# Attention through inducing points with a fused expert layer: a shared maximum per group, exp read from PSUM, a running maximum, and a list scheduler for the order of the work

## The chip, the core and the metric

The kernel runs on one core of a Trainium2 chip. Its engines are TensorE (PE, matrix products; the loads of its weights are listed as PEld), VectorE (DVE), ScalarE (ACT), GpSimd (POOL) and SyncE (SP, which issues DMAs). [...] The metric is the device time of one execution in microseconds (us); less is better.

## The reference

```python
B, N, C, m = 4, 11456, 128, 32        # x: (B, N, C), inducing: (m, C), float32
def mab(q, kv):
    s = q @ kv.T / sqrt(C)
    a = exp(s - s.max(-1)); a /= a.sum(-1) + 1e-9
    return a @ kv
h   = mab(inducing, x)                # first softmax: 32 queries over N tokens, per batch
y   = mab(x, h)                       # second softmax: each token over the 32 rows of h
e   = argmax(y @ w_gate)              # 8 experts, F = 1024 hidden units
out = softmax(y @ w_gate)[e] * (relu(y @ w1[e]) @ w2[e])     # per token
```

A token's `y` is a positive mixture of the 32 rows of `h`. Where every row agrees on the expert and on the sign of each hidden unit, relu(y @ w1[e]) @ w2[e] is linear in the mixture, and one 32x128 matrix per batch (`h4`) replaces the expert. The kernel tests this token by token (a sum of the second softmax's weights against a threshold `thr`) and counts the tokens that fail.

## The kernel before

The tokens of a batch lie in 4 quarters (q), each cut into 90 blocks of 32; 15 blocks of all four quarters make a group (a tile of 128 partitions x 480 columns), 6 groups a batch, 24 groups in all. Of each group the kernel loads `xt` (tokens along the columns, 0.98 MB, L180) and `xn` (tokens along the partitions, L186); for three groups of batch 0 it makes `xn` out of `xt` on TensorE (`turn_xn`). Both loads are issued by SP, the results (0.98 MB a group) by ACT (L496).

First softmax, per group: `attend1` multiplies `xt` with the inducing points into PSUM (L117, four column tiles), DVE transposes the scores in 32x32 blocks into SBUF (L217) and takes their maximum (L218). After all six groups `maxima` joins the maxima (two products) into one per inducing point. Then `attend2` subtracts it (L245, POOL; DVE for batch 0), takes exp (L249, ACT) and sums with 15 products (L258) into one bank `hp` over the whole batch. `induced` divides, finds the expert, and gathers its `w1` and `w2` by an indirect DMA of POOL (L310); `fused` makes `h4` (64 + 256 instructions of small products, L331, L353) and `thr`.

Second softmax, per group k: `scores` (L117); `less_max` (transpose L404, maximum of each token L406, subtraction on POOL L407); `exps` (L412); `logits` (transpose back L416, one product L418 with a matrix that gives the sum of the weights and the gate sums); `turn_logits` (L424). Per pair of groups, `gate1` to `gate3` alternate between POOL and DVE with one exp on ACT (L431 to L465) and give a factor per token. Then `weigh` multiplies (L470, POOL), `experts` transposes (L475) and multiplies with `h4` (L479, four row tiles into four banks `o`), and `evict` copies the four banks (L493, ACT) and stores.

The order is written by hand: `put(at, fn)` places each step at a tick; a group takes STEP = 6 ticks, `attend1` of batch b+2 and `attend2` of batch b+1 are laid between the groups of batch b, and `induced(0)` with its `fused` and the first `attend1` of batch 1 run before tick 0. At the end the failed tokens are counted (L600 to L613); a slow pass over them follows only if there are any.

Of the kernel before, what the change touches and what calls it, by code (L numbers as in the profile page):

```python
# [29 lines left out]
P = 128  # L31
# [4 lines left out]
GB = 15  # L36
# [17 lines left out]
def attn_moe_kernel(ctx, tc, xT, xn, indT, wg, w1, w2, consts, out):  # L54
# [20 lines left out]
    done_all = const.tile([P, B, NBLK], F32, name="done_all")  # L75
# [10 lines left out]
    def open_pools(st, rest):  # L86

        pl = Pools()

        def pool(name, bufs, **kw):  # L90
            return st.enter_context(tc.tile_pool(name=("r_" if rest else "m_") + name, bufs=bufs, **kw))

        pl.xt = pool("xt", 1 if rest else NXT)
        pl.e2 = pool("e2", 2 if rest else 4)
        pl.et = pool("et", 2)
        pl.small = pool("small", 2)
        pl.wraw = pool("wraw", 1)
        pl.fe = pool("fe", 2, space=PSUM)
        pl.mi = pool("mi", 1, space=PSUM)
        if rest:  # L100
            pl.z = pool("z", 2, space=PSUM)
            pl.o = pool("o", 2, space=PSUM)
            pl.ob = pool("ob", 2)
            pl.hid = pool("hid", 2)
        else:
            pl.hp = pool("hp", 1, space=PSUM)
            pl.o = pool("o", 4, space=PSUM)
            pl.lv = pool("lv", 2)
            pl.xn = pool("xn", 3)
            pl.s1 = pool("s1", 7)  # L110
        return pl


    def score_mm(pl, lhsT, xt_g):
        ps = pl.fe.tile([P, 512], F32, name="fe")
# [4 lines left out]
        return ps  # L120

    def softmax_exp(pl, hT, xt_g, side):

        ps = score_mm(pl, hT[:, 0:M], xt_g)
# [44 lines left out]
    pl = open_pools(main, False)  # L169

# [4 lines left out]
    for s in S:  # L175
        s.xt, s.xn, s.s1 = {}, {}, {}

    def load_xt(b, g):
        t = pl.xt.tile([P, GB, NQ, 32], F32, name="xt")
        nc.sync.dma_start(t, xT[b, g])  # L180
        S[b].xt[g] = t

    def load_xn(b, g, pool=pl.xn):

        t = pool.tile([P, GB, P + 1], F32, name="xn")
        nc.sync.dma_start(t, xn[b, :, g * GB : (g + 1) * GB, :])  # L186
        S[b].xn[g] = t

    def turn_xn(b, g, pool):

        s = S[b]
        t = pool.tile([P, GB, P + 1], F32, name="xn")
        nc.gpsimd.memset(t[:, :, P : P + 1], 1.0)
        s.xn[g] = t
        for k0 in range(0, GB, 4):
            n = min(4, GB - k0)
            ps = pl.o.tile([P, 512], F32, name="o")
            for k in range(n):
                nc.tensor.transpose(
                    ps[:, k * P : (k + 1) * P], s.xt[g][:, k0 + k].rearrange("p q t -> p (q t)"), ident  # L200
                )
            src = ps[:, : n * P].rearrange("p (k c) -> p k c", c=P)
            if k0 % 8 == 0 or b > 0:
                nc.scalar.copy(t[:, k0 : k0 + n, 0:P], src)
            else:
                nc.vector.tensor_copy(t[:, k0 : k0 + n, 0:P], src)
            yield

    def attend1(b, g):

        s = S[b]
        ps = score_mm(pl, it_sb, s.xt[g])
        yield
        if g == 0:
            s.mx1 = pl.small.tile([P, NG], F32, name="mx1")
        s.s1[g] = pl.s1.tile([P, GW], F32, name="s1")
        nc.vector.transpose(s.s1[g], ps[:, :GW])  # L217
        nc.vector.tensor_reduce(s.mx1[:, g : g + 1], ps[:, :GW], AX.X, ALU.max)  # L218

    def maxima(b):  # L220

        s = S[b]
        m1 = pl.small.tile([P, 1], F32, name="m1")
        nc.vector.tensor_reduce(m1, s.mx1, AX.X, ALU.max)
        mq = pl.small.tile([P, NQ], F32, name="mq")
        nc.vector.tensor_scalar_mul(mq, qmask, m1)
        ps = pl.mi.tile([P, 512], F32, name="mi")
        nc.tensor.matmul(ps[:, :NQ], lhsT=fold, rhs=mq, start=True, stop=True)
        yield
        mm = pl.small.tile([P, 1], F32, name="mm")  # L230
        nc.vector.tensor_reduce(mm, ps[:, :NQ], AX.X, ALU.max)
        dg = pl.small.tile([32, 32], F32, name="dg")
        nc.vector.tensor_scalar_mul(dg, ident[:32, :32], mm[:32])
        ps2 = pl.mi.tile([P, 512], F32, name="mi")
        nc.tensor.matmul(ps2[:, :32], lhsT=ones[:32, :], rhs=dg, start=True, stop=True)
        yield
        s.m1b = pl.small.tile([P, 32], F32, name="m1b")
        nc.vector.tensor_copy(s.m1b, ps2[:, :32])  # L238

    def attend2(b, g):  # L240

        s = S[b]
        e1 = blk(s.s1[g])
        side = nc.vector if b == 0 else nc.gpsimd
        side.tensor_tensor(  # L245
            out=e1, in0=e1, in1=s.m1b.unsqueeze(1).to_broadcast([P, GB, 32]), op=ALU.subtract
        )
        yield
        nc.scalar.activation(s.s1[g], s.s1[g], AF.Exp, scale=SCALE)  # L249
        if g == NG - 1:  # L250
            nc.gpsimd.memset(e1[64:128, GB - 1, :], 0.0)
        yield
        if g == 0:
            s.hp = pl.hp.tile([P, 512], F32, name="hp")
        for k in range(GB):
            n = g * GB + k
            j = n % 4
            nc.tensor.matmul(  # L258
                s.hp[32 * j : 32 * j + 32, : P + 1],
                lhsT=e1[:, k, :],  # L260
                rhs=s.xn[g][:, k, :],
                start=(n < 4),
                stop=(n >= NBLK - 4),
            )

    def induced(b):

        s = S[b]
        t = pl.small.tile([P, P + 1], F32, name="hsum")
        nc.scalar.copy(t, s.hp[:, : P + 1])  # L270
        ps = pl.mi.tile([P, 512], F32, name="mi")
        nc.tensor.matmul(ps[:, 0:1], lhsT=fold, rhs=t[:, P : P + 1], start=True, stop=True)
        yield
        rv = pl.small.tile([P, 1], F32, name="rv")
        nc.vector.tensor_scalar_add(rv, ps[:, 0:1], EPS)
        nc.vector.reciprocal(rv, rv)
        nc.vector.tensor_scalar_mul(t[:, :P], t[:, :P], rv)
        ps2 = pl.mi.tile([P, 512], F32, name="mi")
        nc.tensor.matmul(ps2[:, 0:P], lhsT=t[:, :P], rhs=fold, start=True, stop=True)
        yield  # L280
        nc.vector.tensor_copy(hT_all[:, b, :], ps2[:, 0:P])
        ps3 = pl.mi.tile([P, 512], F32, name="mi")
        nc.tensor.matmul(ps3[:, 0:E], lhsT=hT_all[:, b, :], rhs=wg_sb, start=True, stop=True)
        yield
        gs = pl.small.tile([P, E], F32, name="gs")
        nc.vector.tensor_copy(gs, ps3[:, 0:E])
        ps4 = pl.mi.tile([P, 512], F32, name="mi")
        nc.tensor.matmul(ps4[:, 0:E], lhsT=ones, rhs=gs, start=True, stop=True)
        yield

        cs = pl.small.tile([P, E], F32, name="cs")
        nc.vector.tensor_copy(cs, ps4[:, 0:E])
        cm = pl.small.tile([P, 1], F32, name="cm")
        nc.vector.tensor_reduce(cm, cs, AX.X, ALU.max)
        t2 = pl.small.tile([P, E], F32, name="t2")
        nc.vector.scalar_tensor_tensor(
            out=t2, in0=cs, scalar=cm, in1=val8, op0=ALU.is_ge, op1=ALU.mult
        )
        r1 = pl.small.tile([P, 1], F32, name="r1")
        nc.vector.tensor_reduce(r1, t2, AX.X, ALU.max)  # L300
        ix = pl.small.tile([P, 1], F32, name="ix")
        nc.vector.scalar_tensor_tensor(
            out=ix, in0=r1, scalar=-128.0, in1=pcol, op0=ALU.mult, op1=ALU.add
        )
        ii = pl.small.tile([P, 1], I32, name="ii")
        nc.vector.tensor_copy(ii, ix)
        s.w1r = pl.wraw.tile([P, F], F32, name="w1r")
        s.w2r = pl.wraw.tile([P, F], F32, name="w2r")
        for dst, src in ((s.w1r, w1), (s.w2r, w2)):
            nc.gpsimd.indirect_dma_start(  # L310
                out=dst, out_offset=None, in_=src, in_offset=bass.IndirectOffsetOnAxis(ap=ii[:, :1], axis=0)
            )

        oh = pl.small.tile([P, E], F32, name="oh")
        nc.vector.tensor_tensor(out=oh, in0=val8, in1=r1.to_broadcast([P, E]), op=ALU.is_equal)
# [78 lines left out]
    for k in range(0, B * NG, 2):  # L394
        K[k].pair = K[k + 1].pair = Pair()

# [404 lines left out]
```

## Time and profile before

| | before |
|---|---|
| three timed runs | 314.4 us median (312.33 to 315.57) |
| profiled execution | 311.58 us |
| its span, first to last instruction | 309.6 us |
[...]

The page names busy time of engines, which says nothing yet of who waits for whom; the timeline and the tables of waits do. A product of float32 appears as two instructions, so the four products of a group's scores are eight rows. Times in the timeline count from the span's start.

### The profile page before, as it was taken

How to read it: one execution, taken by the hardware profiler on the slowest of the kernel's cores; microseconds unless marked ns; L12 is line 12 of the kernel's file. 1: busy time of each engine (PE TensorE's matmuls, PEld its weight loads, DVE VectorE, ACT ScalarE, POOL GpSimd, SP SyncE). 2: the span in 40 equal slices, each digit the busy share in tenths (PEclk: the TensorE clock that was granted, in tenths of full speed). 3: DMA queues.
4: the chain of work that ended last, by engine and by line, in shares of the span. 5: the costliest groups of instructions: out<-in, count | busy, mean ns of one | idle time of the engine just before them, and what ended most of it. 6: DMA issues, size and time to landing. Idle time of an engine off the chain costs nothing. (4 is left out here: it accounts for less than half of the span.)

```text
span 309.6 us, 4648 instructions
## 1 busy us (share of the span) xinstructions
PE 231.7 (75%) x1771; PEld 106.8 (35%) x1772; DVE 153.3 (50%) x392; ACT 86.5 (28%) x172; POOL 117.5 (38%) x194
## 2 busy tenths in 40 slices
PE   2877725778397779769894899799876995994870
PEld 0536404145032145434421344255332541221330
DVE  0585250853656655633856427533544736545420
ACT  1314000023123041452251320362240601552451
POOL 0000020148513712962616403983535226717510
PEclk9995975899789568776999559756968576597555
DMA  7999994128929985757999531059163330345156
GB/s 288 423 420 421 415 416 196 43 89 300 423 67 377 381 326 211 239 197 309 385 371 385 169 163 60 0 188 386 68 255 125 135 131 2 127 176 207 48 227 244
DMA packets 11549, 72.72 MB, mean 235 GB/s; under 512 B 1536, under 2 KB 1664, under 8 KB 11520
## 3 DMA queue, kind: packets, MB, share of 16 engines
q1 hardware_dynamic: 6480, 44.40, 37.2%
q10 hardware_dynamic: 3888, 23.75, 18.7%
q0 software_dynamic: 1152, 4.19, 3.9%
q8 instruction: 16, 0.26, 0.4%
q14 instruction: 13, 0.11, 0.1%
HBM read 48.75 MB, written 23.59 MB: 234 GB/s over the span
## 5 line engine op out<-in xcount | busy, mean ns | idle before, releaser
L479 PE MATMUL o<-ec,h 32*128 32x480 f32 x192 | 63.6, 897 | 17.9 <-DVE ec L475 12.1
L493 ACT COPY ob<-o 128x480 f32<-128x480 f32 x96 | 48.1, 564 | 57.6 <-PE o L479 54.4
L407 POOL TENSOR_TENSOR e<-e,mx 128x480 f32<-128x480 f32 x24 | 23.8, 993 | 70.3 <-DVE mx L406 46.7
L117 PE MATMUL fe<-xt,it_sb 128*32 128x480 f32 x192 | 35.1, 713 | 8.4 <-DMA it_sb<-in_indT 5.8
L418 PE MATMUL mi<-et,gzb 128*128 128x480 f32 x48 | 32.3, 761 | 10.6 <-DVE et L416 5.8
L117 PE MATMUL fe<-xt,hT_all 128*32 128x480 f32 x192 | 38.8, 642 | 1.2 <-DVE mx L218 0.9
L479 PEld LDWEIGHTS o<-ec,h 32*128 32x128 f32 x192 | 22.9, 259 | 46.4 <-ACT ob L493 21.5
L258 PE MATMUL hp<-xn,s 128*32 128x129 f32 x720 | 32.9, 322 | 4.5 <-ACT s L249 2.5
L258 PEld LDWEIGHTS hp<-xn,s 128*32 128x32 f32 x720 | 26.5, 129 | 20.4 <-issue 10.4
L217 DVE STREAM_TRANSPOSE s<-fe 128x480 f32<-128x480 f32 x24 | 16.2, 675 | 28.6 <-PE fe L117 28.6
L416 DVE STREAM_TRANSPOSE et<-e 128x480 f32<-128x480 f32 x24 | 16.0, 669 | 20.3 <-ACT e L412 20.2
L475 DVE STREAM_TRANSPOSE ec<-e 128x480 f32<-128x480 f32 x24 | 16.1, 673 | 16.5 <-POOL e L470 16.5
L412 ACT ACTIVATE e<-e 128x480 f32<-128x480 f32 x24 | 14.6, 607 | 34.1 <-POOL e L407 34.1
L470 POOL TENSOR_TENSOR e<-e,c 128x480 f32<-128x480 f32 x24 | 23.5, 998 | 0.9
L424 DVE STREAM_TRANSPOSE lv<-mi 128x480 f32<-128x480 f32 x24 | 16.1, 669 | 13.7 <-PE mi L418 13.6
L245 POOL TENSOR_TENSOR s<-s,m1b 128x480 f32<-128x480 f32 x18 | 21.2, 1202 | 4.1 <-DVE m1b L238 4.1
L249 ACT ACTIVATE s<-s 128x480 f32<-128x480 f32 x24 | 14.3, 603 | 27.5 <-POOL s L245 19.8
L331 PE MATMUL mi<-hT_all,w1r 128*128 128x32 f32 x64 | 12.1, 357 | 13.2 <-DMA w1r<-in_w,ii 13.2
L404 DVE STREAM_TRANSPOSE e<-fe 128x480 f32<-128x480 f32 x24 | 15.9, 665 | 6.8 <-PE fe L117 6.6
L431 POOL TENSOR_SCALAR sm<-lv 128x30 f32<-128x30 f32 x12 | 3.8, 320 | 38.8 <-DVE lv L424 27.8
L418 PEld LDWEIGHTS mi<-et,gzb 128*128 128x128 f32 x48 | 8.5, 221 | 28.2 <-DVE et L416 11.4
L331 PEld LDWEIGHTS mi<-hT_all,w1r 128*128 128x128 f32 x64 | 11.6, 280 | 17.0 <-issue 9.8
(103 smaller groups left out, 220.2 us busy)
## 6 DMA issues: line engine op xcount, KB each, us to landing
xt<-in_xT SPq DMA_DIRECT2D x24, 960.0 KB, 9.4
out<-ob ACTq DMA_DIRECT2D x24, 960.0 KB, 4.5
xn<-in_xn SPq DMA_DIRECT2D x21, 967.5 KB, 8.4
csb<-in_consts ACTq DMA_DIRECT2D x1, 134.5 KB
w1r<-in_w,ii POOLq DMA_INDIRECT x4, 4.4
w2r<-in_w,ii POOLq DMA_INDIRECT x4, 6.8
it_sb<-in_indT ACTq DMA_DIRECT2D x1, 16.0 KB, 5.0
wg_sb<-in_wg ACTq DMA_DIRECT2D x1, 4.0 KB, 9.5
```

Source lines behind the costliest of these rows:

```text
L117: nc.tensor.matmul(blk(ps[32 * q : 32 * q + 32, :GW]), lhsT=lhsT, rhs=xt_g[:, :, q, :], start=True, stop=True)
L217: nc.vector.transpose(s.s1[g], ps[:, :GW])
L245: side.tensor_tensor(out=e1, in0=e1, in1=s.m1b.unsqueeze(1).to_broadcast([P, GB, 32]), op=ALU.subtract)
L258: nc.tensor.matmul(s.hp[32 * j : 32 * j + 32, : P + 1], lhsT=e1[:, k, :], rhs=s.xn[g][:, k, :], start=(n < 4), stop=(n >= NBLK - 4),)
L331: nc.tensor.matmul(gp[:, 32 * f : 32 * f + 32], lhsT=s.w1r[:, f * P : (f + 1) * P], rhs=hT_all[:, b, 0:M], start=True, stop=True,)
L407: nc.gpsimd.tensor_tensor(out=blk(w.e2), in0=blk(w.e2), in1=mx.unsqueeze(2).to_broadcast([P, GB, 32]), op=ALU.subtract)
L418: nc.tensor.matmul(K[k].lp[:, :GW], lhsT=S[k // NG].gzb, rhs=et, start=True, stop=True)
L424: nc.vector.transpose(pr.lv[:, k % 2, :], K[k].lp[:, :GW])
L470: nc.gpsimd.tensor_tensor(out=e2, in0=e2, in1=c.unsqueeze(2).to_broadcast([P, GB, 32]), op=ALU.mult)
L475: nc.vector.transpose(ec, w.e2)
L479: nc.tensor.matmul(o[:, :GW], lhsT=s.h4[32 * q : 32 * q + 32, :], rhs=ec[32 * q : 32 * q + 32, :], start=True, stop=True,)
L493: nc.scalar.copy(w.ob[:, q, :], w.o[q][:, :GW])
```

## The change

Function by function: in both softmaxes exp reads the scores straight from PSUM, with the negative maximum as bias, and the scale goes into the 32-row factor (`it_s`, `s.hc`). In the first softmax the maximum runs along: after each group the maxima so far are joined by one small product into free columns of the group's own bank, exp uses that, and the batch's sums in SBUF are rescaled by exp(old - new) as the group's sums are added. `maxima` and the POOL subtraction are gone; the transpose now stands behind exp. In the second softmax all tokens of one quarter of a group share one maximum (columns reduced, then across 32 partitions by a transpose of a broadcast column), with the mean row taken out of `h` first. The weights so stay with the inducing rows along the partitions: the transposes L404, L416 and L475 are gone, and the factor per token is transposed and broadcast instead (`turn_factors`). The gate runs on DVE alone but for its exp: `gate1` has an add and a reciprocal of 30 and a fused minimum-and-multiply of 240 elements, `gate_test` a maximum of 240 and two fused tests of 30, `gate2` a sum of 240, an add, a reciprocal and a multiply of 30. `fused` uses 4 + 8 products and a join in place of 8 + 32.

The order comes from `Plan`: each step is an operation with an engine, an assumed duration, the steps it follows, the buffers that it takes and gives, and a rank; `order` always picks the one that can start earliest by these durations, and the program is written in that order. PSUM is 2 banks `fe` (scores), 2 `ps` (sums, gate sums, the small products of a batch) and 4 `o`.

```diff
+LEAD = 4.5
+BUFS = dict(xt=12, xn=3, ob=2, e1t=2, e1=2, et=5, lv=2, cb=2, fe=2, ps=2, o=4, wraw=1)
...
+class Plan:
+    HOP, TIE = 0.2, 0.01
...
+    def order(self):
...
+            for op in ready:
+                at = free.get(op["engine"], 0.0)
+                for a in op["after"]:
+                    at = max(at, a["end"] + a["lag"] + (self.HOP if a["engine"] != op["engine"] else 0.0))
...
+                    key = (at // self.TIE, op["rank"], op["n"])
+                    if best is None or key < best[0]:
+                        best = (key, at, op)
...
+    def group1(b, g, rank, begin):
...
+        def peak():
...
+            nc.vector.tensor_reduce(m, w.ps[:, :GW], AX.X, ALU.max)
+            nc.vector.tensor_scalar_mul(s.mq[:, g, :], qmask, m)
...
+        def spread():
+            w.pm = w.ps[:, GW : GW + NQ * (g + 1)]
+            nc.tensor.matmul(
+                w.pm,
+                lhsT=fold,
+                rhs=s.mq[:, 0 : g + 1, :].rearrange("p g q -> p (g q)"),
...
+        def lowest():
+            nc.vector.tensor_reduce(s.rn[:, g : g + 1], w.pm, AX.X, ALU.max, negate=True)
...
+        def weights():
...
+            nc.scalar.activation(w.et, w.ps[:, :GW], AF.Exp, bias=s.rn[:, g : g + 1])
...
+        def shrink():
...
+            nc.scalar.activation(w.fc, s.rn[:, g - 1 : g], AF.Exp, scale=-1.0, bias=s.rn[:, g : g + 1])
...
+            nc.vector.transpose(w.e1, w.et)
...
+                nc.vector.scalar_tensor_tensor(
+                    out=s.hs, in0=s.hs, scalar=w.fc, in1=w.hp, op0=ALU.mult, op1=ALU.add
...
+        a0 = plan.add("PE", 1.1, scores, [load], rank, ("fe",), lag=0.1)
...
+        a6 = plan.add("PE", 1.3, sums, [a5] + tokens, rank, ("ps",), ((a5, 0), (tokens[0], 0)), lag=0.1)
...
+    def tokens(b, g0):
...
+        def peak(w):
...
+            nc.vector.tensor_reduce(m, w.ps[:, :GW], AX.X, ALU.max)
...
+            nc.vector.transpose(mt, m.to_broadcast([P, 32]))
...
+            nc.vector.tensor_reduce(w.rn, mt, AX.X, ALU.max, negate=True)
...
+        def weights(w):
...
+            nc.scalar.activation(w.et, w.ps[:, :GW], AF.Exp, bias=w.rn)
...
+            nc.vector.transpose(blk(w.cb), c.unsqueeze(2).to_broadcast([P, GB, 32]))
...
+            nc.gpsimd.tensor_tensor(out=w.et, in0=w.et, in1=w.cb, op=ALU.mult)
...
+            w.b9 = plan.add(
+                "PE", 1.2, lambda w=w: experts(w), [b8, s.h4_op], r, ("o",) * 4, ((w.b4, 0),), lag=0.1
...
+    for op in plan.order():
+        op["fn"]()
```

## Rows read from the trace of the kernel before

**Rows 1.** From the page: the heading, the busy time of each engine with its share of the span, and the total of the DMA engines.

```profile
span 309.6 us, 4648 instructions
...
PE 231.7 (75%) x1771; PEld 106.8 (35%) x1772; DVE 153.3 (50%) x392; ACT 86.5 (28%) x172; POOL 117.5 (38%) x194
...
DMA packets 11549, 72.72 MB, mean 235 GB/s; under 512 B 1536, under 2 KB 1664, under 8 KB 11520
```

**Rows 2.** The five stretches that the text names, by the table of windows of the core: start and end in us, length, then for each engine its busy time and instructions in brackets, the granted TensorE clock as a share of 2.4 GHz, the DMA engines' busy share, and GB/s.

```profile
0.00:58.50 58.50, 35.37 (x349) 20.85 (x350) 26.17 (x74) 8.90 (x16) 2.71 (x11) 0.82 0.83 341
58.50:126.00 67.50, 51.50 (x510) 23.62 (x510) 38.84 (x103) 17.35 (x34) 29.64 (x46) 0.85 0.70 266
126.00:189.00 63.00, 51.69 (x410) 24.07 (x409) 32.11 (x84) 19.58 (x40) 27.17 (x41) 0.76 0.70 268
189.00:251.00 62.00, 53.47 (x392) 25.43 (x391) 30.94 (x82) 21.36 (x43) 32.67 (x50) 0.73 0.42 161
251.00:309.60 58.60, 39.67 (x114) 12.87 (x113) 25.28 (x52) 19.31 (x40) 25.27 (x48) 0.65 0.34 136
```

**Rows 3.** The longest waits of the engines, all of the span: who waited for what, us in total, how often, the longest.

```profile
ACT ob L493 <- PE o L479: 54.4, 18, 8.0
...
ACT pr L452 <- POOL ls L439: 40.7, 11, 7.7
```

**Rows 4.** The same view of the queue of SyncE (SP), which issues the loads: L186 is the load of `xn`.

```profile
SPq L186 <- PE hp L258: 108.5, 16, 41.7
```

**Rows 5.** The way from the first softmax of batch 0 to the first scores of its second one, and the first product with the expert's matrix, from the timeline (start, length, instruction, idle time of its engine before it).

```profile
34.82 0.27 ACT L270 COPY hsum<-hp 128x129 f32<-128x129 f32 x1 [5.71 <-PE hp L258]
...
40.56 1.16 POOL L310 DMA_INDIRECT w1r<-in_w,ii  x1 [11.22 <-DVE go L317]
...
49.71 3.59 PE L331 MATMUL mi<-hT_all,w1r 128*128 128x32 f32 x16 [8.93 <-DMA w1r<-in_w,ii]
...
58.56 1.01 PE L117 MATMUL fe<-xt,hT_all 128*32 128x480 f32 x7 [0.90 <-DVE mx L218]
...
82.63 1.97 PE L479 MATMUL o<-ec,h 32*128 32x480 f32 x4 [6.41 <-DVE ec L475]
```

**Rows 6.** Mean durations of one instruction, from the groups of instructions by line and shape (busy time in us, mean of one in ns; then idle time before them).

```profile
L493 ACT COPY ob<-o 128x480 f32<-128x480 f32 x96 | 48.1, 564 | 57.6 <-PE o L479 54.4 <-DMA out<-ob 2.0 <-ACT ob L493 0.5
...
L470 POOL TENSOR_TENSOR e<-e,c 128x480 f32<-128x480 f32 x24 | 23.5, 998 | 0.9
...
L424 DVE STREAM_TRANSPOSE lv<-mi 128x480 f32<-128x480 f32 x24 | 16.1, 669 | 13.7 <-PE mi L418 13.6
...
L218 DVE TENSOR_REDUCE mx<-fe 128x1 f32<-128x480 f32 x24 | 15.0, 624 | 0.0
L412 ACT ACTIVATE e<-e 128x480 f32<-128x480 f32 x24 | 14.6, 607 | 34.1 <-POOL e L407 34.1
...
L457 DVE TENSOR_REDUCE se<-pr 128x30 f32<-128x240 f32 x12 | 4.8, 398 | 11.6 <-ACT pr L452 11.6
...
L463 DVE RECIPROCAL se<-se 128x30 f32<-128x30 f32 x12 | 4.0, 332 | 4.4 <-POOL se L459 4.4
...
L366 DVE COPY h<-mi 128x128 f32<-128x128 f32 x4 | 1.1, 281 | 6.0 <-PE mi L353 6.0
...
L231 DVE TENSOR_REDUCE mm<-mi 128x1 f32<-128x4 f32 x4 | 0.6, 156 | 1.3 <-PE mi L228 1.2
```

**Rows 7.** The forms of matrix product in two stretches, from the timeline, in order of time: L117 scores, L258 sums of the first softmax, L418 gate sums, L479 products with the expert's matrix.

```profile
84.53 1.83 PE L117 MATMUL fe<-xt,it_sb 128*32 128x480 f32 x8
...
89.80 1.08 PE L258 MATMUL hp<-xn,s 128*32 128x129 f32 x30
...
204.35 1.94 PE L258 MATMUL hp<-xn,s 128*32 128x129 f32 x30
...
220.21 1.09 PE L479 MATMUL o<-ec,h 32*128 32x480 f32 x8 [0.28 <-DVE ec L475]
...
255.19 1.07 PE L418 MATMUL mi<-et,gzb 128*128 128x480 f32 x2 [0.25 <-DVE thr L387]
...
260.33 1.98 PE L479 MATMUL o<-ec,h 32*128 32x480 f32 x8 [1.22 <-DVE ec L475]
...
267.62 1.97 PE L418 MATMUL mi<-et,gzb 128*128 128x480 f32 x2 [0.31 <-DVE et L416]
...
289.54 4.98 PE L479 MATMUL o<-ec,h 32*128 32x480 f32 x8 [0.60 <-ACT ob L493]
```

**Rows 8.** Windows of single products and of two longer stretches; columns as in the five stretches.

```profile
5.00:20.00 15.00, 12.96 (x85) 6.84 (x85) 8.13 (x15) 3.52 (x6) 0.00 (x0) 1.00 1.02 420
84.50:86.30 1.80, 1.80 (x11) 0.22 (x9) 0.61 (x1) 1.02 (x2) 0.00 (x0) 0.50 0.84 345
255.10:256.30 1.20, 1.07 (x2) 0.30 (x2) 0.62 (x2) 0.16 (x1) 0.92 (x3) 1.00 0.00 0
267.60:269.60 2.00, 1.98 (x3) 0.59 (x4) 1.36 (x2) 0.38 (x1) 2.00 (x3) 0.50 0.60 242
55.00:70.00 15.00, 11.56 (x147) 4.90 (x143) 10.12 (x32) 2.41 (x4) 4.97 (x5) 0.94 0.20 68
170.00:190.00 20.00, 18.30 (x120) 8.15 (x124) 8.84 (x33) 4.96 (x11) 4.56 (x5) 0.59 0.41 152
```

**Rows 9.** The end of the program, from the timeline.

```profile
302.87 0.34 ACTq L496 DMA_DIRECT2D out<-ob  x1
```

More of the change, by code (lines that the diff above doesn't have):

```diff
@@ L105, in open_pools, with score_mm @@
         else:
[L106 to L110, printed above, removed]
[L111 to L115 removed]
+            pl.buf = pool("buf", 1)
+            pl.bank = pool("bank", 1, space=PSUM)
+            pl.bat = pool("bat", 2)
+        return pl
+    def score_mm(ps, lhsT, xt_g):
         for q in range(NQ):
@@ L209, in attend1 @@
[L209 to L257, printed above, removed]
-            nc.tensor.matmul(
[L259 to L315, printed above, removed]
-        go = pl.small.tile([P, E], F32, name="go")
-        nc.vector.tensor_tensor(out=go, in0=gs, in1=oh, op=ALU.mult)
-        gst = pl.small.tile([P, 1], F32, name="gst")
-        nc.vector.tensor_reduce(gst, go, AX.X, ALU.add)
-        nc.vector.scalar_tensor_tensor(out=go, in0=oh, scalar=FAR, in1=gs, op0=ALU.mult, op1=ALU.add)
-        nc.vector.tensor_scalar(gz[:, 1 : 1 + E], go, gst, None, op0=ALU.subtract)
-        s.gzb = block_diagonal(pl, gz)
-        start(fused(b), 5)
@@ new lines, in turn_weights, with sums @@
+        def turn_weights():
+            w.e1 = buf(a5)
+            nc.vector.transpose(w.e1, w.et)
+            if g == NG - 1:
+                nc.gpsimd.memset(blk(w.e1)[64:128, GB - 1, :], 0.0)
+        def sums():
+            w.hp = buf(a6)[:, : P + 1]
+            for k in range(GB):
+                j = k % 4
+                nc.tensor.matmul(
+                    w.hp[32 * j : 32 * j + 32, :],
+                    lhsT=blk(w.e1)[:, k, :],
+                    rhs=w.xn[:, k, :],
+                    start=(k < 4),
+                    stop=(k >= GB - 4),
+                )
@@ L583, in attn_moe_kernel @@
-    pl.ob = main.enter_context(tc.tile_pool(name="m_ob", bufs=2))
-    for g in range(3):
-        load_xn(1, g)
-    now(induced(0))
-    for g in range(NG):
-        start(attend1(1, g))
-        tick()
-    start(maxima(1))
-    last = max(plan)
-    t = 0
-    while t <= last or running:
-        for fn, a in plan.get(t, ()):
-            fn(*a)
-        tick()
-        t += 1
-    nc.vector.memset(done_all[64:128, :, NBLK - 1 : NBLK], 1.0)
+                    w.gp[32 * j : 32 * j + 32, 0 : F // 4],
@@ new lines, in mm_h4, with copy_h1 @@
+        def mm_h4():
+            w.p3 = buf(f4)
+            for f in range(NF):
+                j = f % 4
+                nc.tensor.matmul(
+                    w.p3[32 * j : 32 * j + 32, 0:P],
+                    lhsT=w.gl[:, f, :],
+                    rhs=w.w2r[:, f * P : (f + 1) * P],
+                    start=(f < 4),
+                    stop=(f >= NF - 4),
+                )
+        def copy_h1():
+            w.h1 = pl.bat.tile([P, P], F32, name="h1")
+            nc.vector.tensor_copy(w.h1, w.p3[:, 0:P])
```

666 lines of the change are left out of this document (400 added, 266 removed).

## The prediction

> **What bounds the kernel now.** I read the page's first part, then five stretches, the waits, and last the timeline where an engine stands still. No engine is full: PE is busy 231.7 of 309.6 us, DVE 153.3, POOL 117.5, ACT 86.5, and the 72.72 MB of the DMAs would take 173 us at the 420 GB/s that one early window holds [rows 1, 8]. What fills the span is order. Before 58.5 us PE works 35 us; the last 58.6 us, with one batch's second softmax left, hold 39.7 us of PE at a clock of 0.65 and 25 us of DVE [rows 2]. The reader should see three things.
>
> First, the start: the sums of batch 0 end at 34.8, the gather starts at 40.6, PE stands 8.9 us for `w1`, the first scores of the second softmax come at 58.6 and the first product with `h4` at 82.6 [rows 5]. The scores need `h` alone; they come late because the program lists them behind `fused`, on an engine that works in order. Second, the gate passes between POOL and DVE: ACT stands 40.7 us for one result of POOL's gate [rows 3]. Third, products and copies wait for each other: ACT waits 54.4 us for products, and one group's eight instructions with `h4` take 1.98 us where four banks are free and 4.98 where they come back one by one [rows 3, 7]. SP's `xn` loads wait 108.5 us for sums to free buffers [rows 4], so the DMAs rest too (share 0.34 to 0.42 in the last two stretches [rows 2]).
>
> **The change, part by part.** *DVE.* I cost each instruction by its nearest row [rows 6]. First softmax, a group: maximum 0.62, multiply 0.16, negative maximum 0.16, transpose 0.67, adding the sums 0.28: 1.89 us. Second softmax, a group: maximum 0.62, two small steps of 0.16, two transposes: 2.28. Gate of a pair: three passes of 240 elements at 0.40, two reciprocals at 0.33, five small ones at 0.16: 2.66, or 1.33 a group. Together 5.5 x 24 = 132 us. A batch's small chain has some 40 instructions, most of 0.16 to 0.28, a few wider: 9 us, x 4 = 36. Six copies of the turned `xn` (0.6 each, as ACT's copy of 0.56) 4. That is 172; neighbours overlap a little in the records, so I take 165. Three transposes a group leave, but POOL's gate, the running maximum and the rescaled sums come, so DVE grows from 153 to 165 (bounds 153 and 172) and becomes the busiest engine for its length. The steps that no row shows (a transpose of a broadcast, the fused passes) lie between 0.16 and 0.67 each; with 24 such transposes at 0.16 the sum falls by 12.
>
> *POOL* keeps 24 multiplications of 1.0 us [rows 6] and the gathers. Nothing of its saving counts by itself; it counts as a shorter chain. *ACT*: two exps of 0.61, four copies of 0.56, about 0.3 of small exps a group, 3.8 x 24 = 91 us, under DVE's work everywhere. An exp from PSUM has no row; the copies from PSUM are of 0.56 [rows 6], so it should lie between 0.56 and 0.7, hidden under DVE.
>
> *PE.* [...] With turning and the batches' products (20 us) PE's work is about 157 us at the high and 265 at the low level. The two levels, not the instructions removed, decide PE's part: `fused` goes from 40 products a batch to 13, but at 3.59 us for the eight with `w1` [rows 5] that is a few us a batch, and only batch 0's stand in the way of others.
>
> *The order.* Group sums of batch 0 now run as groups land: the last of nine loads (8.9 MB at 420 GB/s, 21 us after the first 2.5) lands at 24, 3 more since only three `xn` buffers exist and its load waits for a group's sums. One group's chain follows: 1.0 + 0.78 + 0.4 + 0.16 + 0.61 + 0.67 + 1.1 + 0.28 = 5.0, with seven handovers of 0.1 5.7, then division and centring 2.3. The first scores of the second softmax can start at 35 in place of 58.6 (bounds 31, and 58.6 if the order held them back). The gather starts near 36, and the row shows 9.1 us from its issue to the first product with `w1` [rows 5]; with 5 us for `fused`, the first `h4` product comes near 52 in place of 82.6. PE is covered in between by six first-softmax groups of batch 1 and up to five groups of scores (`et` has five buffers). If that cover failed, 17 us would show. New waits are on in-order queues: a `h4` product that waits for four free banks holds scores and sums behind it on PE, and a DVE step that waits for ACT's gate exp holds the next maximum, thus the next exp.
>
> *The sum.* From 35 us on DVE has 165 - 20 = 145 us left. Its best long window now is 10.12 of 15 us, 0.67; PE's best is 18.30 of 20, 0.91 [rows 8]. At these shares the body takes 216 or 159. I take 0.76, nearer to DVE's own, since DVE gets still more short dependent steps: 191. PE agrees: 137 us left at the high level, over a mean clock of 0.80 (between the 0.85 and 0.76 of the second and third stretch [rows 2]) and a share of 0.9, is 190. After the last DVE step come multiplication 1.0, products 2.0, four copies 2.3, and from the last store's issue to the end 6.7 [rows 9]: 12. So 35 + 191 + 12 = 238, against 309.6. Outside the span lie 2.0 us (311.58 against 309.6): 240. The median of the runs shown is 0.9% above the profiled execution; with that, 242.
>
> [...] The row: from 170 to 190 us PE is busy 18.3 of 20 us at a granted clock of 0.59 [rows 8], so a busy PE in the records was not a fast one; there its `h4` products waited for banks. [...]
>
> The row: eight `h4` instructions took 4.98 us when banks came back one by one, the four copies of a group being 4 x 0.56 = 2.3 us of ACT [rows 6, 7]. [...]
>
> **The rivals.** *The order closes nearly all gaps.* Body at a share of 0.91: 35 + 159 + 12 + 2 = 208; the DMAs' 173 us and the tail allow it. For it speaks that early windows hold DMA at 420 GB/s under PE and DVE work [rows 8]; against it that no stretch so far keeps two engines above 0.85.
>
> *The ladder of banks stays and PE remains slow.* If `h4` products keep waiting for copies, the clock stays at the last stretch's 0.65 [rows 2]: 137/0.65/0.9 = 234, plus 35, 12 and 2: 283. For it: the assumed durations (1.1, 1.2, 1.3 for products) are those of the high level, so a low clock puts the written order out of step. Against: products are placed where four banks should be free, with sums and scores in between.
>
> *Slower: pairs run one after the other.* If each pair's gate must end before PE and DVE get the next pair's steps in their queues, a pair costs its chain: scores 1.83, maximum 0.94, exp 0.61, gate sums 1.97, transpose 0.67, 2 more for its second group, gate 3.0, factors 0.67, multiplication 1.0, products and copies twice 4.2, handovers 1.2: 22.3 us. 52 + 12 x 22.3 + 12 + 2 = 334. It decides from 20.4 us a pair on, (311 - 66)/12. For it: in-order queues and an order from guessed durations; against: five `et` and two `lv` buffers let three pairs overlap.
>
> *The saving ends up in other waits,* within a few per cent of before: the head's 24 us would have to be given back; I see no row for that. The slow pass does not start: worked out from the reference's inputs, the smallest sum of weights with shared maxima is 31.995 and the thresholds are at most 31.980.
>
> **How the numbers follow.** About 1% is what a measurement of this kernel can tell from no change. Chances: forecast 0.46 (226 to 258), gaps closed 0.25 (200 to 226), ladder 0.20 (258 to 300), unchanged within 1% 0.02, faster by little 0.02, slower 0.05. Predicted 242. The range 205 to 285 holds the forecast, four fifths of the second case and over half of the third, 0.8 in all. Faster by over 1%: 0.93; within: 0.02; slower: 0.05.
>
> **What would show it.** Right: first L117-type scores of the second softmax near 35, first `h4` product near 52; DVE 155 to 172 us busy and near 0.7 of the span; POOL under 40; eight `h4` instructions in 1.1 to 2.0 us, not 4 or 5; a clock of 0.8 or more; no `xn` load waiting tens of us. Wrong: DVE transposes of a broadcast or exps from PSUM far from 0.67 and 0.61; a clock still near 0.65 in the second half; ACT waiting for products as long as before; or scores of batch 0 held back behind the gather.

## The result and the profile after

The changed kernel takes 270.6 us (median of four runs, 268.2 to 274.67) against 314.99 us for the kernel before in the same session: a ratio of 0.854 (95% interval 0.844 to 0.865), a gain of 44 us. That lies in the range given, 29 us above the predicted value. Some runs of a kernel take over 1.5% longer than its fastest; the ratios, and the differences in us between kernels from here on, leave them out, so that the changed kernel counts as 268.4 us. The page, where the first and last lines answer to [rows 1]:

```profile
span 266.7 us, 4317 instructions
...
PE 187.1 (70%) x1583; PEld 82.3 (31%) x1584; DVE 157.8 (59%) x528; ACT 89.6 (34%) x184; POOL 37.2 (14%) x44
...
DMA packets 11548, 72.69 MB, mean 273 GB/s; under 512 B 1536, under 2 KB 1664, under 8 KB 11520
```

The bytes are the same, POOL lost two thirds of its work, and PE's busy time fell by 44.6 us: it has fewer instructions (1583 for 1771), and the mean granted clock rose from 0.763 to 0.859 (shares of full speed; no trace here gives the clock in GHz, as the line of [rows 2] has it). PE's idle time did not shrink (the span less its busy time: 77.9 us before, 79.6 after), so on PE the whole gain of 42.9 us in the span is shorter busy time. 19 us of it are in the products with `h4`, the same 192 instructions, and 15 in the fewer products with `w1` and `w2`. First the kernel before, then the changed one (busy us and mean ns of one, then idle time before):

```profile
L479 PE MATMUL o<-ec,h 32*128 32x480 f32 x192 | 63.6, 897 | 17.9 <-DVE ec L475 12.1 <-ACT ob L493 5.6
...
L331 PE MATMUL mi<-hT_all,w1r 128*128 128x32 f32 x64 | 12.1, 357 | 13.2 <-DMA w1r<-in_w,ii 13.2
L353 PE MATMUL mi<-w2r,gl 128*32 128x128 f32 x256 | 10.7, 337 | 1.1 <-issue 0.6 <-DVE gmn L370 0.5
```

```profile
L655 PE MATMUL o<-et,h 32*128 32x480 f32 x192 | 44.4, 732 | 19.9 <-POOL et L651 17.4 <-ACT ob L666 2.4
...
L480 PE MATMUL ps<-w1r,hT_all 128*32 128x256 f32 x32 | 4.5, 570 | 13.7 <-DMA w1r<-in_w,ii 13.7
L507 PE MATMUL ps<-w2r,gl 128*32 128x128 f32 x64 | 3.3, 336 | 1.2 <-DVE gl L499 1.2
```

Cut where the prediction cut it (head to the first scores of the second softmax, body to the end of the last factor transpose, tail), the table of windows reads as follows; columns as in [rows 2].

```profile
0.00:43.40 43.40, 30.28 (x314) 18.23 (x316) 19.94 (x55) 10.06 (x20) 0.56 (x9) 0.90 0.91 352
43.40:250.80 207.40, 151.09 (x1253) 61.24 (x1252) 135.08 (x468) 75.67 (x156) 34.60 (x34) 0.88 0.68 262
250.80:266.70 15.90, 5.76 (x18) 2.84 (x18) 2.80 (x5) 3.89 (x8) 1.99 (x2) 0.50 0.47 191
```

Head 43.4 (forecast 35), body 207.4 (191), tail 15.9 (12): together 28.7 us over the forecast span of 238. In the body neither PE (0.73) nor DVE (0.65) is full. PE's waits say what it lacked, the wait of ACT's copies for products is shown with them, and the groups say what the new steps cost (busy us and mean ns, then idle time before and what ended it; rows of before for the same work: [rows 3, 6]):

```profile
ACT ob L666 <- PE o L655: 57.1, 17, 14.6
...
PE o L655 <- POOL et L651: 17.4, 8, 4.5
...
PE ps L480 <- DMA w1r<-in_w,ii: 13.7, 2, 9.4
PE fe L351 <- DVE mq L347: 6.8, 6, 2.4
...
PE fe L191 <- DMA xt<-in_xT: 4.5, 1, 4.5
...
PE o L655 <- ACT ob L666: 2.4, 3, 0.9
```

```profile
L651 POOL TENSOR_TENSOR et<-et,cb 128x480 f32<-128x480 f32 x24 | 28.4, 1203 | 135.3 <-DVE cb L648 118.3 <-DVE keep L497 13.8 <-ACT fc L368 2.0
...
L595 ACT ACTIVATE et<-fe,rn 128x480 f32<-128x480 f32 x24 | 16.0, 668 | 31.9 <-DVE rn L591 27.5 <-PE ps L480 3.4 <-PE o L655 0.5
...
L648 DVE STREAM_TRANSPOSE cb<-c_all 128x480 f32<-128x480 f32 x24 | 14.9, 656 | 0.6
L351 PE MATMUL fe<-mq,csb 128*128 128x4 f32 (+5 forms) x48 | 9.3, 268 | 7.2 <-DVE mq L347 6.8 <-DVE ix L452 0.4
```

The ladder of banks is weaker: the mean product with `h4` takes 732 ns for 897, in which the higher clock has a part (eight such instructions took 1.09 us at a granted clock of 1.00, from 233.48 us, and 1.98 at 0.50, from 100.05). It still shows where two groups stand close together, as at 206.29 us, where a group's eight instructions take 3.97 us, at a mean granted clock of 0.79, while its banks come back one by one. ACT's copies wait as long for products as before (57.1 us for 54.4 [rows 3]). What the `h4` products themselves wait for before they start is now POOL's product, 17.4 us. PE's timeline near the end shows that this wait holds up others:

```profile
206.29 3.97 PE L655 MATMUL o<-et,h 32*128 32x480 f32 x8 [0.72 <-ACT ob L666]
...
233.48 1.09 PE L655 MATMUL o<-et,h 32*128 32x480 f32 x8 [2.62 <-POOL et L651]
234.50 1.88 PE L599 MATMUL ps<-et,gzb 128*128 128x480 f32 x4
236.31 1.01 PE L191 MATMUL fe<-xt,hc 128*32 128x480 f32 x8
237.25 1.09 PE L655 MATMUL o<-et,h 32*128 32x480 f32 x8
242.28 1.60 PE L655 MATMUL o<-et,h 32*128 32x480 f32 x8 [3.94 <-POOL et L651]
243.81 1.97 PE L599 MATMUL ps<-et,gzb 128*128 128x480 f32 x2
245.71 1.35 PE L655 MATMUL o<-et,h 32*128 32x480 f32 x8
251.59 1.18 PE L655 MATMUL o<-et,h 32*128 32x480 f32 x4 [4.53 <-POOL et L651]
```

PE waits from 238.3 for a factor; the gate sums (L599) that are listed behind the waiting product start at 243.81, the next pair's gate starts behind them on DVE, and so its factor is late again. The sums' own input, an exp on ACT, ends at 240.86, so they are held up by 3 us, not by all of the wait:

```profile
240.16 0.70 ACT L595 ACTIVATE et<-fe,rn 128x480 f32<-128x480 f32 x1
```

From 233.5 to 251.6 a pair takes 9 us. The products with `w1` (L480) do the same with the gathered rows: 9.4 us in batch 2.

### The profile page after: what moved, and what is told of

Its sections match the earlier page's. It is cut to its first block, busy times and chain, and to the rows that moved or that the text cites. A ratio compares the mean times of both kernels' runs of the same rounds, so it can differ in the third digit from the quotient of the medians.

```text
span 266.7 us, 4317 instructions
## 1 busy us (share of the span) xinstructions
PE 187.1 (70%) x1583; PEld 82.3 (31%) x1584; DVE 157.8 (59%) x528; ACT 89.6 (34%) x184; POOL 37.2 (14%) x44
## 4 chain that ended last, share of the span: by engine, by line
PE 43%; DVE 29%; DMA 14%; ACT 4%; issue 4%; POOL 3%; ACTq 0%; POOLq 0%; DVEq 0%
PE fe L191 11%; PE o L655 11%; DMA w1r<-in_w,ii 7%; PE ps L380 7%; PE ps L599 5%; DMA xt<-in_xT 3%; DVE cb L648 3%; POOL et L651 3%; DVE e L372 3%; DMA csb<-in_consts 3%; PE o L300 3%; DVE mx L587 3%; DVE lv L603 2%; PE fe L351 2%; DVE mx L346 2%
## 5 line engine op out<-in xcount | busy, mean ns | idle before, releaser
L666 ACT COPY ob<-o 128x480 f32<-128x480 f32 x96 | 47.5, 570 | 57.7 <-PE o L655 57.1
L655 PE MATMUL o<-et,h 32*128 32x480 f32 x192 | 44.4, 732 | 19.9 <-POOL et L651 17.4
L651 POOL TENSOR_TENSOR et<-et,cb 128x480 f32<-128x480 f32 x24 | 28.4, 1203 | 135.3 <-DVE cb L648 118.3
L191 PE MATMUL fe<-xt,it_s 128*32 128x480 f32 x192 | 31.5, 666 | 13.1 <-DVE it_s L152 6.2
L380 PE MATMUL ps<-xn,e 128*32 128x129 f32 x720 | 33.6, 308 | 6.3 <-DVE e L372 4.2
L191 PE MATMUL fe<-xt,hc 128*32 128x480 f32 x192 | 35.5, 642 | 0.2 <-ACT et L595 0.2
L380 PEld LDWEIGHTS ps<-xn,e 128*32 128x32 f32 x720 | 25.2, 122 | 24.4 <-DVE e L372 10.9
L599 PE MATMUL ps<-et,gzb 128*128 128x480 f32 x48 | 27.1, 652 | 5.5 <-ACT et L595 4.1
L364 ACT ACTIVATE e1t<-fe,rn 128x480 f32<-128x480 f32 x24 | 15.9, 663 | 42.3 <-DVE rn L360 40.8
L655 PEld LDWEIGHTS o<-et,h 32*128 32x128 f32 x192 | 14.6, 213 | 42.4 <-POOL et L651 29.2
L595 ACT ACTIVATE et<-fe,rn 128x480 f32<-128x480 f32 x24 | 16.0, 668 | 31.9 <-DVE rn L591 27.5
L603 DVE STREAM_TRANSPOSE lv<-ps 128x480 f32<-128x480 f32 x24 | 16.1, 671 | 15.4 <-PE ps L599 15.3
L346 DVE TENSOR_REDUCE mx<-fe 128x1 f32<-128x480 f32 x24 | 15.5, 645 | 14.7 <-PE fe L191 12.6
L587 DVE TENSOR_REDUCE mx<-fe 128x1 f32<-128x480 f32 x24 | 15.5, 645 | 9.0 <-PE fe L191 8.9
L351 PE MATMUL fe<-mq,csb 128*128 128x4 f32 (+5 forms) x48 | 9.3, 268 | 7.2 <-DVE mq L347 6.8
L480 PE MATMUL ps<-w1r,hT_all 128*32 128x256 f32 x32 | 4.5, 570 | 13.7 <-DMA w1r<-in_w,ii 13.7
L599 PEld LDWEIGHTS ps<-et,gzb 128*128 128x128 f32 x48 | 7.6, 198 | 19.8 <-ACT et L595 9.4
L351 PEld LDWEIGHTS fe<-mq,csb 128*128 128x128 f32 x48 | 7.8, 199 | 16.0 <-DVE mq L347 10.6
```

The costliest lines, as they stand in the source:

```text
L191: nc.tensor.matmul(blk(ps[32 * q : 32 * q + 32, :GW]), lhsT=lhsT, rhs=xt_g[:, :, q, :], start=True, stop=True)
L346: nc.vector.tensor_reduce(m, w.ps[:, :GW], AX.X, ALU.max)
L351: nc.tensor.matmul(w.pm, lhsT=fold, rhs=s.mq[:, 0 : g + 1, :].rearrange("p g q -> p (g q)"), start=True, stop=True,)
L380: nc.tensor.matmul(w.hp[32 * j : 32 * j + 32, :], lhsT=blk(w.e1)[:, k, :], rhs=w.xn[:, k, :], start=(k < 4), stop=(k >= GB - 4),)
L587: nc.vector.tensor_reduce(m, w.ps[:, :GW], AX.X, ALU.max)
L599: nc.tensor.matmul(w.lp[:, :GW], lhsT=s.gzb, rhs=w.et, start=True, stop=True)
```

## The experiments

Two theories were tried. **One:** the gain comes from the parts with shorter chains and the scheduler only adds a little. **Two:** what is missing against the forecast is lost at the head of PE's queue, where a product that must wait has ready work behind it. A rival for the second was that the loads come late (SP waits 92.5 us for `xn` buffers).

### Where the gain comes from

The scheduler undone: each operation gets a tick by hand, and the list is sorted by it.

```diff
-                    key = (at // self.TIE, op["rank"], op["n"])
+                    key = (self.tick(op), op["n"])
```

> The changed operations and buffers, but the order by ticks like those of the kernel before (six ticks a group, each step at a fixed tick after its group's first) in place of the earliest start by assumed durations. Theory A (the order carries the gain): 290 us or more, at least half of the 44 us given back. Theory B (the shorter chains carry it): 280 or less.

Measured 279.97 us (274.06 to 290.99), ratio 0.883 (0.871 to 0.895): 7 us lost, theory B.

The shared maximum undone, under the scheduler: transposes, one maximum for each token, and POOL's subtraction are back.

```diff
-            nc.vector.tensor_reduce(m, w.ps[:, :GW], AX.X, ALU.max)
+            nc.vector.transpose(w.e2, w.ps[:, :GW])
+            nc.vector.tensor_reduce(w.mx, blk(w.e2), AX.X, ALU.max)
...
+                out=blk(w.e2), in0=blk(w.e2), in1=w.mx.unsqueeze(2).to_broadcast([P, GB, 32]), op=ALU.subtract
```

> The second softmax with a maximum for each token again (scores transposed to SBUF, subtraction on POOL, exp in SBUF, transposes before the gate sums and before the h4 product), five e2 buffers; first softmax, gate and list scheduler as changed. DVE gains about 1 us a group (2.65 in place of 1.67), so 24 us, to 181 us busy; POOL 24 us. Theory A (the order carries the gain): 270 to 282, since DVE was idle 40% of the span. Theory B (the removed operations carry it): 290 or more.

Measured 275.98 us (269.05 to 278.47), DVE 181.1 and POOL 55.9 us busy. Only the run of 269.05 can be set against 268.4, so there is no interval; no loss is shown, although DVE has 23 us more to do. Theory B is out. Then both edits together:

> Undoes two parts together: the maximum of each token in the second softmax again (three transposes a group and a subtraction on POOL) and the order by hand-set ticks. The changed kernel took 270.6, either part undone alone 276 and 280. Theory A: the two parts are worth the sum of what each is worth alone, so 283 to 288, and the remaining 27 us or so of the gain belong to the running maximum, the exp from PSUM and the shorter start. Theory B: each part covers for the other, since the scheduler hides longer chains and short chains forgive a poor order; both undone then cost clearly more than the sum, 293 or more.

Measured 302.91 us, ratio 0.964 (0.955 to 0.973): 35 us lost, where the two lose 7 us between them when undone alone. The second theory of that expectation holds: each part covers for the other. All other parts together, with an order by ticks, are worth the remaining 11 us against 314.35.

### The running maximum

Its undoing: ACT copies the scores to SBUF (seven buffers), and exp of all six groups waits for the sixth maximum.

```diff
+            nc.scalar.copy(w.et, w.ps[:, :GW])
...
-            nc.scalar.activation(w.et, w.ps[:, :GW], AF.Exp, bias=s.rn[:, g : g + 1])
+            nc.scalar.activation(w.et, w.et, AF.Exp, bias=s.rn[:, NG - 1 : NG])
```

> Undoes the running maximum alone: scores of a first-softmax group are copied from PSUM to SBUF by ACT (0.57 us a group more), and exp of all six groups waits for the maximum of the sixth; no rescaling of the sums. The scheduler orders it. Theory A: the running maximum carries most of what is left of the gain: the first scores of the second softmax come at 52 or later in place of 43.4, the xn loads wait behind the barrier in every batch, and the time is 285 or more. Theory B: the scheduler covers the barrier in batches 1 to 3 and only the head of batch 0 is longer, by 3 to 8 us: 273 to 279.

Measured 257.04 us, ratio 0.815 (0.808 to 0.823). Both theories were wrong in sign: the kernel is 11 us faster without the running maximum. Its body by the table of windows, and, by the groups of instructions, the one join that is left of each batch:

```profile
49.00:238.90 189.90, 146.52 (x1170) 60.65 (x1163) 129.85 (x442) 73.47 (x145) 34.66 (x34) 0.87 0.70 267
```

```profile
L354 PE MATMUL fe<-mq,csb 128*128 128x24 f32 x8 | 1.8, 308 | 2.2 <-DVE mq L350 2.2
```

The head is 5.6 us longer (first scores at 49.0), which is what the running maximum saves; the body is 17.5 us shorter. PE spends 1.8 + 2.2 us on joins and on waiting for them, where the changed kernel spends 9.3 + 7.2 (L351 above). PE's busy time in all is no shorter for it, 187.5 us for 187.1; what fell is its idle time, 67.7 for 79.6, with the wait for POOL's product down from 17.4 to 5.1 us. This pair alone does not part the joins from the new order. A rival was the PSUM bank that a group holds through maximum, join and exp. It was taken away while the joins stayed: the same copy to SBUF, exp per group, the join in a bank of its own.

```diff
-            w.pm = w.ps[:, GW : GW + NQ * (g + 1)]
+            w.pm = buf(a2)[:, : NQ * (g + 1)]
...
+            nc.scalar.copy(w.et, w.ps[:, :GW])
```

> The running maximum stays, with its join after each group and the rescaled sums, but ACT copies the scores of a first-softmax group to SBUF as with the barrier (seven buffers), so that their PSUM bank is free after the maximum and the copy; the join's small product goes to one of the two ps banks. The barrier in place of the running maximum gave 257.0, the changed kernel 270.6. Theory A: what the running maximum costs is the bank that a group holds through its chain (maximum, join, negative maximum, exp): with the scores held in SBUF 255 to 262. Theory B: it costs by the join itself, 24 small products that stand in PE's queue and wait for DVE, and by the longer chain: 265 to 275.

Measured 270.14 us, ratio 0.859 (0.849 to 0.868): not to be told from the changed kernel. With a copy more on ACT, which is busy 103.5 of 269.2 us here, the held bank cannot be seen in the time. PE's idle time is shorter, 61.9 us for 79.6, but the same 1583 instructions took 207.3 us for 187.1, at a granted clock of 0.823 for 0.859. So theory B has the number, but that the join and its chain are the cost is not shown. (All these kernels were ordered anew, so a part of the barrier's 11 us may be the order; see the last pair below.)

### Buffers for the loads

```diff
-BUFS = dict(xt=12, xn=3, ob=2, e1t=2, e1=2, et=5, lv=2, cb=2, fe=2, ps=2, o=4, wraw=1)
+BUFS = dict(xt=12, xn=5, ob=2, e1t=2, e1=2, et=5, lv=2, cb=2, fe=2, ps=2, o=4, wraw=1)
```

> Five xn buffers in place of three. Theory A: SP waits 92.5 us for sums to free an xn buffer, with xt loads listed behind; group 5 of batch 0 is late (first scores of the second softmax at 43 and not 35 us) and PE waits 4.5 us for an xt load near 115 us. With five buffers the first scores come at 36 to 40 us and the time falls by 4 to 9 us, to 262 to 267. Theory B: the order only shifts the loads, the 72.7 MB take their 173 us, and PE is held by other things: within 3 us of 270.

Measured 290.27 us, ratio 0.932 (0.921 to 0.943): both theories wrong, 22 us slower. The planner, given more buffers, lists groups of batch 1 ahead of batch 0's second softmax, whose first scores come at 52.3. To part the buffers from the order, five buffers were run in the order found for three:

```diff
+XN = 5
...
+    def follow(self, seq):
+        self.units = {k: list(range(n)) for k, n in dict(BUFS, xn=XN).items()}
```

> Five xn buffers in place of three, but the operations stay in the order that the planner found for three, on every engine but for a few loads of SP. Five buffers with a new order took 290.3. Theory A: that loss was the new order (batch 1's groups were put ahead of batch 0's second softmax, whose first scores came at 52.3 for 43.4), and the buffers themselves help: SP's waits for xn buffers fall from 92 us to under 50, first scores near 42, time 262 to 270. Theory B: the loss was the early traffic of the loads, which take bandwidth from what is needed first: 278 or more, with the first scores late again.

Measured 272.69 us, ratio 0.865 (0.855 to 0.874): not to be told from the changed kernel, so the loss was the order, and the gain that was hoped for is not there either. SP's waits, first in the changed kernel, then here:

```profile
SPq L336 <- PE ps L380: 92.5, 16, 17.5
...
SPq L289 <- PE fe L191: 30.3, 7, 13.0
```

```profile
SPq L303 <- PE fe L205: 94.5, 12, 24.4
SPq L350 <- PE ps L394: 36.2, 8, 8.5
```

The wait moved from the `xn` to the `xt` loads. First scores came at 42.4, 1 us earlier. The late loads are not what the head or the body lacks.

### The head of PE's queue

The gather's landing, assumed 12 us in place of 7 (the changed kernel's trace has 4.4 to 10.8 for `w1`, behind a POOL issue of 0.98), so that `w1` products are listed later:

```diff
-        i5 = plan.add("POOL", 1.0, gather, [i4], r, ("wraw",), lag=7.0)
+        i5 = plan.add("POOL", 1.0, gather, [i4], r, ("wraw",), lag=12.0)
```

> One number of the changed kernel: the order assumes that the gathered matrices are there 12 us after the gather's issue, not 7. Nothing else. Theory A: over the forecast stands above all PE's in-order queue, blocked at 90 to 99 us and 149.7 to 160.7 us by the product with w1, which the order places too early for batches 1 and 2 (waits of 4.3 + 9.4 us on PE, and slow clock behind them). Then the two waits fall below 3 us in all and the time falls by 8 to 15 us, to 256 to 263. Theory B: DVE (158 us) and the chains of the pairs bound the kernel anyway: PE then waits elsewhere and the time stays within 3 us of 270.

Measured 265.22 us, ratio 0.851 (0.845 to 0.858), between the two theories. PE's waits for `w1` are gone, 13.7 us, but the time falls by 3 us at most (1 us by the ratios), and the intervals overlap: no gain is shown. PE's idle time fell by 12.0 us and its busy time rose by 9.6. With the barrier in place of the running maximum the same edit gave nothing:

> The barrier of the run that gave 257.0 together with the assumed landing of the gather of 12 us in place of 7. In that run PE still waited 16.3 us for gathered rows. Theory A: the two gains add, the waits for gathered rows fall under 3 us and the time is 249 to 254. Theory B: a new order gives back elsewhere what that wait cost: 255 to 262.

Measured 257.71 us, ratio 0.816 (0.804 to 0.829), theory B. Nor did the planner need better durations (two of its edits; beside those that the expectation names, the gather's issue and the adding of the sums were set too):

```diff
-        a1 = plan.add("DVE", 0.8, peak, [a0], rank)
+        a1 = plan.add("DVE", 0.95, peak, [a0], rank)
...
-                "PE", 1.2, lambda w=w: experts(w), [b8, s.h4_op], r, ("o",) * 4, ((w.b4, 0),), lag=0.1
+                "PE", 1.5, lambda w=w: experts(w), [b8, s.h4_op], r, ("o",) * 4, ((w.b4, 0),), lag=0.1
```

> The gather's assumed landing of 12 us, and beside it the planner's assumed durations set to those of the changed kernel's trace (maximum 0.95 and 1.05 for 0.8 and 0.95, exp 0.68 for 0.62, gate sums 1.3 for 1.1, products with h4 1.5 for 1.2, multiplication on POOL 1.25 for 1.0, gate steps 1.05, 0.85, 1.1 for 0.85, 0.7, 0.9, division 1.7 for 0.9). With the landing alone it was 265.2. Theory A: the order is out of step with the chip because its durations were guessed too short; with measured ones the waits shrink and the time is 256 to 262. Theory B: the durations matter little beside the order in which loads and batches are picked: 262 to 272.

Measured 266.82 us, ratio 0.846 (0.840 to 0.853), theory B again, although in its profile (an execution of 274.32 us) the wait for POOL's product is down to 6.0 us. Then this wait was taken on by itself. The product on POOL gets an assumed lag of 4 us, which changes no operation, only the order:

```diff
-            b8 = plan.add("POOL", 1.0, lambda w=w: weigh(w), [w.b7], r, give=((w.b7, 0),))
+            b8 = plan.add("POOL", 1.0, lambda w=w: weigh(w), [w.b7], r, give=((w.b7, 0),), lag=4.0)
```

> The changed kernel with the gather's assumed landing of 12 us (265.2 alone) and the result of POOL's multiplication assumed 4 us later than it is modelled, so that the products with h4 are listed behind gate sums and scores that are ready before them. In the changed kernel PE waited 17.4 us for POOL's result with gate sums of the next group listed behind, and from 222 us on each pair's gate so waited for the h4 products of the pair before. Theory A: these waits at the head of PE's queue set the pace of the last batch: they fall under 7 us and the time is 254 to 261. Theory B: the pace is set by the chain itself, not by the place in the queue: 262 to 270.

Measured 249.5 us, ratio 0.792 (0.776 to 0.809): 16.7 us faster than with the landing alone, with intervals that lie apart, and below the range of theory A. Windows of head, body and tail, and PE's waits:

```profile
0.00:42.20 42.20, 28.10 (x315) 17.04 (x317) 19.81 (x55) 10.05 (x20) 0.56 (x9) 0.93 0.92 358
42.20:225.90 183.70, 147.97 (x1245) 59.98 (x1244) 135.60 (x458) 71.19 (x147) 34.47 (x33) 0.89 0.75 286
225.90:246.70 20.80, 11.14 (x26) 5.25 (x26) 6.50 (x16) 8.35 (x17) 2.46 (x2) 0.55 0.59 240
```

```profile
PE ps L480 <- DMA w1r<-in_w,ii: 7.3, 1, 7.3
...
PE o L655 <- POOL et L651: 3.0, 5, 1.0
```

The wait for POOL falls from 17.4 us (15.8 with the landing alone) to 3.0. DVE does the same 135 us of work in the body as in the changed kernel, in 184 us in place of 207. The last run, the three edits above together, tells whether the barrier won by itself or by such an order, and whether the lag helps a second kernel:

> The barrier in place of the running maximum, the gather's assumed landing of 12 us and POOL's result assumed 4 us later, all three. Without the barrier that was 249.5; the barrier with the landing alone 257.7. Theory A: the running maximum costs by its own work, 24 joins in PE's queue and a longer chain a group, whatever the order; without it 238 to 245. Theory B: the barrier won only because its order happened to keep products with h4 from waiting at the head of PE's queue, which the assumed lag now does for either; the time is 246 to 253, the barrier's later start of batch 0's second softmax (49.0 for 43.4) cancelling what the joins cost.

Measured 243.61 us, ratio 0.768 (0.757 to 0.778), in the range of theory A, and the fastest kernel here. The lag is worth 15.4 us with the barrier and 16.7 without. The barrier is worth 11.3, 8.2 and 6.9 us in the three pairs, the last with intervals that touch: part of the 11.3 may be the order.

What the lag works by is less plain than its worth. By the profiles (us; idle is the span less PE's busy time; the last column is PE's wait for POOL's product):

| kernel | span | PE busy | PE idle | granted clock | wait for POOL |
|---|---|---|---|---|---|
| changed | 266.7 | 187.1 | 79.6 | 0.859 | 17.4 |
| landing of 12 | 264.3 | 196.7 | 67.6 | 0.843 | 15.8 |
| landing, measured durations | 272.6 | 209.5 | 63.1 | 0.801 | 6.0 |
| landing, lag | 246.7 | 187.2 | 59.5 | 0.865 | 3.0 |
| barrier, landing | 256.6 | 188.3 | 68.3 | 0.822 | 9.3 |
| barrier, landing, lag | 242.4 | 182.9 | 59.5 | 0.849 | 4.8 |

With the barrier the lag took only 4.5 us from that wait, and the span fell by 14.2. With the measured durations the wait fell by 9.8 us and no time was won, while the same 1583 instructions took 209.5 us for 196.7 at a granted clock of 0.801 for 0.843 (0.819 to 0.828 in this kernel's other runs, 265.9 to 267.86 us). So the order that the lag gives is shown to be better, in two kernels; that it is better by this one wait is not. No run here shows why the clock held with the lag and fell without it.

## Why the forecast was right, and where it was 29 us short

**Right.** Shorter chains and the scheduler pay together; no engine became full. DVE 157.8 (forecast 165, bounds 153 and 172), ACT 89.6 (91), POOL 37.2 (under 40), exp from PSUM 0.66 to 0.67 (0.56 to 0.7), the joins 0.39 us a group (0.4), the broadcast transpose 0.656 (0.67, not the 0.16 of its lower bound). The slow pass did not start. The clock was better than forecast, 0.86 for 0.80 and 0.88 in the body, so the clock is not why the time was above the forecast. Nor does the clock go with PE's idle time alone in these runs: PE stood idle as long as before at a higher clock (79.6 us at 0.859, 77.9 at 0.763), and less, 61.9 to 67.6 us, at 0.801 to 0.843 with the landing, the measured durations and the scores held in SBUF. The prediction's 157 and 265 us of PE work, and the 137 us that its check by PE and the ladder use, were the author's estimate: 24 groups at 5.7 and 10.0 us and the batches' products, from what the forms took before at a granted clock of 1.00 (scores twice 1.01, sums 1.08, gate sums 1.07, `h4` products 1.09 us) and of 0.50 (1.83 to 1.98 for the same forms), with a guess for the joins (0.4 us at the higher one). No run shows PE's work at one such clock throughout; the changed kernel shows 187.1 us at a mean of 0.859.

**By luck.** 270.6 lies in the part of the range, 258 to 300, that the prediction gave to the ladder of banks with a chance of 0.20. That rival's mechanism was weak here (a group's eight `h4` instructions took 1.09 to 3.97 us, and the clock was 0.79 over the last 66.7 us, not 0.65), so the range held the result for another reason than the one that made it wide. One of the signs of being wrong did come: ACT waits for products as long as before, 57.1 us. And of the signs of being right several failed: DVE is at 0.59 of the span, not near 0.7, and SP still waits 92.5 us for sums to free `xn` buffers, 17.5 us at the longest.

**The step that failed** is in the sum: "I take 0.76" for DVE's share of the body. It measured 0.65 (135.08 of 207.4). No row stood behind 0.76; the best long window of before had 0.67. DVE's work in the body was 10 us below the 145 us assumed; at 0.76 that would be 178 us. The check by PE failed at the same place: its share of the body was 0.73, not 0.9. The prediction named a wait of this kind, "a `h4` product that waits for four free banks holds scores and sums behind it on PE", but with the wrong releaser: most of the wait is for POOL's product, 17.4 us, and 2.4 for banks. With the order that the assumed lag gives, DVE's share is 0.74 (135.60 of 183.7), and the body is 7 us under the forecast's. So the share was within reach of an order; which waits keep it from there is shown only in part (see the table above). The rival of pairs in series was real for the last pairs alone, at 9 us each and not 22.3.

**The running maximum** was priced as 0.4 us of PE a group, which was right, and as sums that run as groups land, which is worth 5.6 us of head. What the sum lacked is any cost in the body: the joins also wait 6.8 us for DVE, and the kernel without them is faster in all three pairs. How much of that is the joins and how much the order stays open.

**The head, 8.4 us.** The forecast let group sums run "as groups land". With `xn` early the first scores still came at 42.4, so late `xn` loads are not the cause. By the timeline the sixth group's scores start at 31.2 (forecast 27), behind other sums on PE; its sums are added by 38.5, 7.3 us for the chain where 5.7 were assumed; and division and centring end at 42.9, 4.5 us where 2.3 were assumed. The first `h4` product at 66.94 (forecast 52) turned out to measure little: it came at 74.3 to 77.6 in five faster kernels.

**The tail, 3.9 us.** The last products ran after waits, at a clock of 0.50, and it took 8.5 us from the last store's issue to the end of the span where [rows 9] led to 6.7.

**Not settled.** Why the scheduler and the shared maximum cover for each other so fully is read from three times, not traced to one wait. Whether the landing alone gains anything is open too. A single new order can move the time by more than the edit that it was made for, as the five buffers show (290.27 and 272.69 us), so only differences that came back in a second pair, the lag and in sign the barrier, are called shown, and they are shown of the edit with its order, not of one wait.

## What to carry to other kernels

Price a new step not only by its duration but by what is listed behind it: in the changed kernel PE stood 3.94 us before the product with `h4` at 242.28 us, and gate sums whose input was there at 240.86 started at 243.81. Assuming a late result in the planner (4 us here) was worth 15 to 17 us in two kernels, with no operation changed. A wait that is removed is not time won: in three edits here PE's idle time fell by 12 to 18 us and its busy time rose by 10 to 22. A scheduler's order is part of every experiment, so freeze it when a buffer is tested, and repeat an edit on a second kernel before its gain is believed. A barrier that costs 5.6 us once in the head was cheaper here, in three pairs, than small handovers in every group.

## What the runs showed of the hardware

Two small DVE steps that were stretched while POOL multiplied, in the changed kernel:

```profile
165.77 1.19 POOL L651 TENSOR_TENSOR et<-et,cb 128x480 f32<-128x480 f32 x1 [13.84 <-DVE keep L497]
168.12 1.21 POOL L651 TENSOR_TENSOR et<-et,cb 128x480 f32<-128x480 f32 x1 [1.16 <-DVE gmn L535]
```

```profile
165.91 1.33 DVE L499 TENSOR_TENSOR gl<-gT,keep 128x256 f32<-128x256 f32 x1
168.18 1.18 DVE L347 TENSOR_SCALAR mq<-csb,mx 128x4 f32<-128x4 f32 x1
```

The same instructions take 0.42 and 0.23 us at the median; the stretched ones end 0.28 and 0.03 us after POOL's. That POOL's work is the cause is not shown beyond these two.

In the changed kernel POOL's multiplication takes 1203 ns with a dense second operand, where [rows 6] have 998 for one that is broadcast along the innermost 32 (the kernel before, with 32 values repeated block by block in the subtraction at L245, took 1202). The four gathers of `w1` in the changed kernel land 4.4 to 10.8 us after their issue.
